# The low halves of FFN 1's first four weight blocks formed in PSUM, in a kernel with attention and two feed-forward nets

## The chip, the cores and the metric

The kernel runs on one core of a Trainium2 chip. The metric is the time of one execution in microseconds of device time, the median of the runs shown. The core has five engines with queues of their own: TensorE (PE in the profile, with its weight loads as PEld), VectorE (DVE), ScalarE (ACT), GpSimd (POOL) and SyncE (SP), which here only starts transfers. Each works through its own list in order, and waits at an instruction until what it needs is there.

## The reference

Attention over a sliding window, then two feed-forward nets, all in float32. What is computed, cut to what matters:

```python
# q, k, v: (4, 8, 576, 64); window 128, causal, with a slope per head
scores = scale * q @ k.T + slope[h] * -(abs(i - j))        # where 0 <= i - j < 128
attn = exp(scores - max) / (sum + 1e-9)
x = (attn @ v)            # laid out as 2304 tokens x 512
# FFN 1: w_in (512, 1024), w_out (1024, 512)
h = x @ w_in
solu = h * softmax(h)
ln = (solu - mean) / sqrt(var + 1e-6) * g_ln
y = ln @ w_out
# FFN 2: w_gate, w_val (512, 1536), w_out (1536, 512)
g = y @ w_gate
out = (g * sigmoid(g) * (y @ w_val)) @ w_out
```

## The kernel before

The weights of both nets arrive as float64 words and are decoded on the chip. For the big products every float32 operand is split into a high half (rounded to the type float32r, in which TensorE takes a 512-column product in one pass) and a low half (what the rounding left over). A product is then three passes: low by high, high by low, high by high (HALVES).

The tokens are worked in 18 chunks of 128 (numbered 0 to 17), and attention in each chunk in four pairs of heads. For a chunk and pair the steps are: `score` (line 518, TensorE), the row maxima with the bias (L571, VectorE), the exponentials (L597 for the chunks below SUMS, L606 for the others, ScalarE), for the chunks from SUMS on the division by the row sums (L576 and L577 on VectorE, L584 on GpSimd), the turning of the probabilities (L657, TensorE, for the chunks below TURN; through a DMA from TURN on), the copies out of PSUM (L667 on VectorE, L670 on ScalarE), and the products with the values (L705, TensorE). For the chunks below SUMS TensorE also spreads the inverse sums (L713), and ScalarE and VectorE multiply with them (L735, L738). Then the chunk's x is split (L318 on ScalarE, L324 on GpSimd or L322 on VectorE).

FFN 1 stands in `up` (L798, names shared, 24 matmuls of 512 columns for a chunk), its statistics (L821, L829 to L849, with the exponentials L832 and the squares L840 on ScalarE), `flip` (L903, eight transposes for a chunk, or through a DMA) and `down1` (L798, names wout and lnT). The weights of FFN 1 come in eight blocks each of w_in and w_out. `decode` makes one: ScalarE turns the two words of each number (L356, L360), VectorE shifts and joins them (L361, L362), GpSimd adds (L364), ScalarE or VectorE rounds to the high half (`high`, L318 or L319), and VectorE or GpSimd subtracts to get the low half (`low`, L322 or L324). A block is held in one of two buffers named db until its low half is made. For w_out there is a multiplication with g_ln between (L373). FFN 2 follows with L1169 (gate and value) and L1348 (output), from about 293 us to the end.

The order in which each engine's instructions stand is made by a planner in the kernel (the class Emitter) when the program is built: every step has a rank (the chunk's number plus an offset such as O_SPL or PW_IN), every way of doing it an engine and a planned cost, and the planner takes the step with the lowest rank among those that are ready in its own reckoning. B_DVE, B_ACT and the values ending in 0 shift steps between VectorE, ScalarE and GpSimd. The constants at the top of the file (lines 48 to 88) thus set the order of the whole program.

## Time and profile before

| | |
|---|---|
| time before, median of 3 runs | 717.71 us (716.42 to 717.73) |
| the profiled execution | 716.97 us, of which the span is 715.0 us |
| PE busy | 690.8 us, 97% of the span |
| PEld busy | 626.5 us, 88% |
| DVE, ACT, POOL busy | 559.4, 427.6 and 271.9 us |
| granted TensorE clock, mean | 0.995 |
| chain that ended last | PE 82%, DMA 8%, DVE 4% |

The span goes from the first instruction to the last. A busy PE need not be working at its full pace: the ends of matmuls are modelled in this view. In the rows further on, an arrow in an operation reads out of the right into the left (`pt<-bank`), `xN` is the number of records, and brackets hold the idle time before a row and what ended it.

### The profile page before, as it was taken

To read this page: it belongs to the slowest core of one execution; us is meant where nothing else is said; L and a number is where in the kernel's file an instruction comes from. 1 tells how busy PE (TensorE), PEld (TensorE's weight loads), DVE (VectorE), ACT (ScalarE), POOL (GpSimd) and SP (SyncE) were. 2 spreads that over 40 slices of the span, in tenths; PEclk is the share of its full clock that TensorE was granted. 3 is DMA by queue.
4 is the path that set the end of the run, shared out by engine and by line. 5 is a ranking of instruction groups with operands and counts; after the bars stand their busy time and mean duration, and the time that the engine had idled before them with its cause. 6 is when DMAs were issued, how large, how long until landed. Compare 5 with 4: busy or idle time off the path is not lost.

```text
span 715.0 us, 14190 instructions
## 1 busy us (share of the span) xinstructions
PE 690.8 (97%) x5060; PEld 626.5 (88%) x5060; DVE 559.4 (78%) x1458; ACT 427.6 (60%) x1019; POOL 271.9 (38%) x280
## 2 busy tenths in 40 slices
PE   3889999999999999999999999999999999999997
PEld 1666777788788888899999999999999999999997
DVE  6979995778877469968778677697794799886966
ACT  7899985755676357855565566465553663443432
POOL 2666899889987314700132132122210001200100
PEclk9999999999999999999999999999999999999999
DMA  9952158978878453437535445545441996886951
GB/s 315 352 159 65 46 147 214 249 207 197 190 188 181 86 147 97 125 92 139 185 130 172 145 155 162 171 161 185 155 148 54 370 378 220 262 287 204 311 166 67
DMA packets 113319, 130.24 MB, mean 182 GB/s; under 512 B 65632, under 2 KB 77920, under 8 KB 113248
## 3 DMA queue, kind: packets, MB, share of 16 engines
q1 hardware_dynamic: 112832, 128.87, 59.6%
q8 instruction: 40, 0.66, 0.4%
q10 hardware_dynamic: 416, 0.46, 0.2%
q14 instruction: 31, 0.25, 0.1%
HBM read 75.57 MB, written 39.06 MB: 160 GB/s over the span
## 4 chain that ended last, share of the span: by engine, by line
PE 82%; DMA 8%; DVE 4%; POOL 2%; ACT 2%; issue 1%; SPq 1%; ACTq 0%; POOLq 0%; DVEq 0%
PE bank L1169 32%; PE bank L798 26%; PE bank L1348 18%; PE bank L705 3%; PE bank L518 2%; DMA dw<-w 2%; DMA dw<-w_in 1%; DMA t<-yscr 1%; DMA dw<-w_out 1%; DMA keys<-qk 1%; PE bank L903 1%; DMA tables<-tables 1%; POOL shared L324 1%; POOL db L364 1%; PE bank L657 1%
## 5 line engine op out<-in xcount | busy, mean ns | idle before, releaser
L1169 PE MATMUL bank<-yt,w 128*128 128x384 f32 x1008 | 185.8, 337 | 0.4 <-ACT set L1191 0.4
L1169 PEld LDWEIGHTS bank<-yt,w 128*128 128x128 f32 x1008 | 176.2, 188 | 1.9 <-ACT set L1191 0.8
L364 POOL TENSOR_TENSOR db<-db,dw 128x512 int32<-128x512 int32 x52 | 73.7, 1419 | 204.4 <-DVE db L362 168.4
L1348 PE MATMUL bank<-w,wo 128*128 128x384 f32 x756 | 132.9, 337 | 1.2 <-POOL w L324 1.2
L1348 PEld LDWEIGHTS bank<-w,wo 128*128 128x128 f32 x756 | 132.3, 188 | 1.6 <-POOL w L324 1.6
L798 PE MATMUL bank<-wout,lnT 128*128 128x512 f32 x432 | 102.5, 391 | 0.0
L1169 PE MATMUL bank<-shared,w 128*128 128x384 f32 x504 | 97.2, 337 | 0.8 <-ACT set L1196 0.5
L798 PEld LDWEIGHTS bank<-wout,lnT 128*128 128x128 f32 x432 | 80.5, 188 | 16.8 <-issue 0.4
L1169 PEld LDWEIGHTS bank<-shared,w 128*128 128x128 f32 x504 | 88.4, 188 | 1.4 <-ACT set L1196 0.8
L798 PE MATMUL bank<-shared,shared 128*128 128x512 f32 x288 | 77.9, 406 | 0.9 <-POOL shared L324 0.6
L798 PEld LDWEIGHTS bank<-shared,shared 128*128 128x128 f32 x288 | 52.6, 191 | 14.4 <-issue 2.7
L606 ACT ACTIVATE e<-e,st 128x128 f32<-128x128 f32 x96 | 37.5, 400 | 22.9 <-DVE st L571 17.9
L318 ACT CAST w<-t 128x384 fp32r<-128x384 f32 (+2 forms) x35 | 26.3, 770 | 37.5 <-DVE t L1292 23.7
L356 ACT ACTIVATE dw<-dw 128x512 int32<-128x512 uint32 x52 | 34.8, 676 | 13.3 <-DMA dw<-w 11.0
L1203 ACT ACTIVATE set<-set 128x384 f32<-128x384 f32 x34 | 17.8, 525 | 40.3 <-DVE set L1201 40.3
L310 POOL COPY pl<-e 128x512 uint16<-128x512 uint16 (+1 forms) x50 | 39.9, 823 | 0.4
L322 DVE TENSOR_TENSOR w<-db,w 128x512 fp32r<-128x512 f32 (+1 forms) x48 | 30.7, 646 | 11.4 <-ACT w L318 11.0
L518 PE MATMUL bank<-keys,raw 64*32 64x160 f32 (+3 forms) x1152 | 30.0, 313 | 9.9 <-DMA raw<-qk 6.3
L361 DVE TENSOR_SCALAR db<-db 128x512 uint32<-128x512 uint32 x52 | 29.9, 576 | 11.7 <-ACT db L360 11.7
L798 PE MATMUL bank<-shared 128*128 128x512 f32 x144 | 38.7, 390 | 0.0
L362 DVE SCALAR_TENSOR_TENSOR db<-dw,db 128x512 uint32<-128x512 uint32 x52 | 36.9, 712 | 0.8
L318 ACT CAST w<-db 128x512 fp32r<-128x512 f32 (+1 forms) x45 | 25.4, 566 | 16.6 <-POOL db L364 7.3
(134 smaller groups left out, 1232.9 us busy)
## 6 DMA issues: line engine op xcount, KB each, us to landing
dw<-w SPq DMA_DIRECT2D x36, 512.0 KB, 4.6
t<-ascr SPq DMA_DIRECT2D x21, 768.0 KB, 6.0
ascr<-set SPq DMA_DIRECT2D x34, 384.0 KB, 2.9
later<-ascr SPq DMA_DIRECT2D x15, 768.0 KB, 6.0
wo<-wscr SPq DMA_DIRECT2D x6, 896.0 KB, 8.6
lscr<-pl SPq DMA_DIRECT2D x20, 256.0 KB, 2.9
v<-v SPq DMA_DIRECT2D x18, 256.0 KB, 3.6
yscr<-ys SPq DMA_DIRECT2D x18, 256.0 KB, 2.3
```

The lines of the kernel that those rows point to most:

```text
L310: (POOL, 100.0 + 1.72 * n, lambda: nc.gpsimd.tensor_copy(dst, words))]
L318: return [(ACT, t_act(n, sbuf), lambda: nc.scalar.copy(hi, src)), (DVEP if sbuf else DVE, t_dve(n, sbuf), lambda: nc.vector.tensor_copy(hi ...
L322: ways = [(DVEP if sbuf else DVE, t_dve(n), lambda: nc.vector.tensor_sub(lo, src, hi.bitcast(F32)))]
L356: r = yield (ACT, 48 + t_act(512), lambda: nc.scalar.activation(a, lw, AF.Copy, scale=2.0 ** -29), (), 0.0, O_DEC)
L361: x = yield (DVEP, t_dve(512, True), lambda: nc.vector.tensor_scalar(b, b, 3, None, ALU.logical_shift_left), [x], 0.0, O_DEC)
L362: x = yield (DVEP, t_dve(512), lambda: nc.vector.scalar_tensor_tensor(b, hw, 0x80000000, b, ALU.bitwise_and, ALU.bitwise_or), [x], 0.0, O_DEC)
L364: x = yield (POOL, 1290, lambda: nc.gpsimd.tensor_tensor(b.bitcast(I32), b.bitcast(I32), a, ALU.add), [x, r], 0.0, O_DEC)
L518: nc.tensor.matmul(banks[ks[r]][i:i + Q, j * 256 + o:j * 256 + o + w], raw[c][rows, 2 * qd + j, i:i + Q], kt[rows, 2 * qd + j, k0:k0 + w], ...
L606: ex.append((yield (ACT, 68 + 75 * j + t_act(P, True, True), lambda j=j: nc.scalar.activation(e[0:n, j], e[0:n, j], AF.Exp, bias=st[0:n, j ...
L798: nc.tensor.matmul(o, terms[m][0], terms[m][1], start=(m == 0), stop=(m == len(terms) - 1))
L1169: nc.tensor.matmul(o, l, r, start=first and m == 0, stop=m == 5, skip_group_check=True)
L1348: nc.tensor.matmul(o, w[:, b], ob[k, i][a][:, j], start=i == 0 and m == 0, stop=i == HB - 1 and m == 2)
```

## The change

Four of the eight blocks of w_in get their low half in another way. TensorE multiplies the decoded float32 block by the identity into a PSUM bank, and adds minus the identity times the high half; the bank then holds the low half, and ScalarE or VectorE copies it out. The planner leaves the choice between these two engines to its costs; it chose ScalarE for all four. One small tile `minus` is made once from the identity. The block's buffer is given back when TensorE has read it. All the constants that set the order are new.

```diff
-SUMS = 6
-TURN = 9
+SUMS = 5
+TURN = 10
-WHOLE = 10
+WHOLE = 9
-VB = 3
-PW_2 = -9.573
+VB = 4
+PW_2 = -11.369
...
+O_LO = -0.25
+BY_PE = 4
...
-    def decode(hi, lo, src, scale=None, even=False):
+    def decode(hi, lo, src, scale=None, even=False, by_pe=False):
...
         x = yield (high(hi, bf, 512), [x], 0.0, O_SPL)
+        if by_pe:
+            k = yield bank_s
+
+            def rest():
+                nc.tensor.matmul(banks[k], ident, bf, start=True, stop=False)
+                nc.tensor.matmul(banks[k], minus, hi, start=False, stop=True)
+
+            x = yield (PE, 1080, rest, [x] + minus_ok, 0.0, O_LO)
+            em.give(db_s, x)
+            x = yield ([(DVE, t_dve(512), lambda: nc.vector.tensor_copy(lo, banks[k])),
+                        (ACT, t_act(512, False), lambda: nc.scalar.copy(lo, banks[k]))], [x], 0.0, O_SPL)
+            em.give(bank_s, x, k)
+            yield x
+            return
         ways = low(lo, bf, hi, 512)
...
+    minus = at.tile([P, P], F32R, name="minus")
...
-                    yield from decode(win[0][:, r, cs], win[1][:, r, cs], w_in[r * P:(r + 1) * P, cs])
+                    yield from decode(win[0][:, r, cs], win[1][:, r, cs], w_in[r * P:(r + 1) * P, cs], by_pe=half * KM + r < BY_PE)
```

In the changed file the lines stand 2 lower from line 371 on and 20 lower behind the new code: L320 is the old L318, L358 and L362 the old L356 and L360, L538 the old L518, L617 the old L597, L677, L690, L725, L733 and L818 the old L657, L670, L705, L713 and L798. L382 and L383 are the two new matmuls, L388 is the new copy out of the bank, L465 makes `minus`.

SUMS moves chunk 5 to the other way of dividing by the sums, TURN moves the turning of chunk 9 from the DMA to TensorE. Over the whole program TensorE gets 8 more transposes (L657, 72 to 80), 8 fewer products with the sums (L713, 48 to 40) and the 8 new matmuls; VectorE makes 1 of w_in's low halves instead of 4 and GpSimd 3 instead of 4; VectorE also loses its 3 of the 16 bias tiles (L462), 5 of 6 copies L671 and 2 casts L319 of w_in, all to ScalarE. The two halves of a chunk's scores stand back to back 3 times instead of 11 times.

Here is TensorE's list behind the first scores (bank is PSUM, tables holds the identity, e the probabilities, db a decoded block, shared the halves of w_in and x, pt the turned probabilities). Before:

```order
32 L518 MATMUL bank_82<-keys,raw 32x128
33 L657 MATMUL bank_83<-tables,e 128x128 x2
34 L657 MATMUL bank_86<-tables,e 128x128 x2
35 L657 MATMUL bank_79<-tables,e 128x128 x2
36 L705 MATMUL bank_80<-pt,v 64x128 x4
37 L657 MATMUL bank_83<-tables,e 128x128 x2
38 L518 MATMUL bank_84<-keys,raw 32x160
```

And with the change:

```order
33 L382 MATMUL bank_80<-db,tables 128x512
34 L383 MATMUL bank_80<-shared_73,minus 128x512
35 L677 MATMUL bank_86<-tables,e 128x128 x2
36 L677 MATMUL bank_82<-tables,e 128x128 x2
37 L725 MATMUL bank_83<-pt,v 64x128 x4
38 L677 MATMUL bank_80<-tables,e 128x128 x2
39 L677 MATMUL bank_86<-tables,e 128x128 x2
```

The first low half stands ahead of the first turning; the other three stand between the scores of chunks 1 to 3, all ahead of the first `up`.

Next is ScalarE's list at its start (dw the words of a block, bias the bias tiles, rs the row sums). Before:

```order
6 L461 ACTIVATE bias<-tables 128x128 x13
7 L597 ACTIVATE e,rs<-e,st 128x128 x3
8 L356 ACTIVATE dw<-dw 128x512
9 L670 COPY pt<-bank_83 128x256
10 L360 ACTIVATE db<-dw 128x512
11 L597 ACTIVATE e,rs<-e,st 128x128 x3
12 L670 COPY pt<-bank_86 128x256
13 L597 ACTIVATE e,rs<-e,st 128x128 x2
14 L356 ACTIVATE dw<-dw 128x512
```

And with the change:

```order
6 L481 ACTIVATE bias<-tables 128x128 x2
7 L465 ACTIVATE minus<-tables 128x128
8 L481 ACTIVATE bias<-tables 128x128 x11
9 L320 CAST shared_73<-db 128x512
10 L481 ACTIVATE bias<-tables 128x128 x3
11 L358 ACTIVATE dw<-dw 128x512
12 L362 ACTIVATE db<-dw 128x512
13 L617 ACTIVATE e,rs<-e,st 128x128 x3
14 L388 CAST shared_74<-bank_80 128x512
15 L690 COPY pt<-bank_86 128x256
16 L617 ACTIVATE e,rs<-e,st 128x128 x2
```

All the bias tiles, the first high half and the first copy of a low half now stand in ScalarE's list among the first exponentials.

Last, TensorE's list up to the turning of chunk 6's fourth pair, the 28th pair to be turned (ident is the identity, e_948 a chunk of FFN 1). Before:

```order
325 L713 MATMUL bank_83<-tables,rs 64x128 x8
326 L657 MATMUL bank_84<-tables,e 128x128 x2
327 L657 MATMUL bank_79<-tables,e 128x128 x2
328 L657 MATMUL bank_86<-tables,e 128x128 x2
329 L798 MATMUL bank_81<-shared_73,shared_74 128x512 x2
330 L798 MATMUL bank_81<-shared_73 128x512 x4
331 L657 MATMUL bank_79<-tables,e 128x128 x2
332 L903 MATMUL bank_83<-ident,e_948 128x128 x4
```

And with the change:

```order
360 L725 MATMUL bank_85<-pt,v 64x128 x2
361 L725 MATMUL bank_85<-pt,vd 64x128 x2
362 L725 MATMUL bank_85<-pt,v 64x128 x2
363 L818 MATMUL bank_81<-shared_74,shared_73 128x512 x4
364 L818 MATMUL bank_81<-shared_73,shared_74 128x512 x2
365 L677 MATMUL bank_82<-tables,e 128x128 x2
366 L677 MATMUL bank_87<-tables,e 128x128 x2
367 L818 MATMUL bank_81<-shared_73,shared_74 128x512 x2
```

The same turning stands at row 331 before and at row 366 now: more of TensorE's work, 18 more matmuls of `up` among it, stands ahead of it.

## Rows read from the trace of the kernel before

**Rows 1.** Busy us per stretch: PE, PEld, DVE, ACT, POOL, then clock and DMA.
```profile
60.00:90.00 30.00, 29.33 (x369) 22.37 (x369) 28.76 (x117) 29.18 (x92) 22.70 (x25) 1.00 0.19 55
...
320.00:610.00 290.00, 287.53 (x1641) 285.39 (x1641) 226.78 (x405) 159.89 (x304) 51.91 (x41) 1.00 0.55 184
```

**Rows 2.** Timeline of all engines at the 28th turning (start us, length us).
```profile
83.84 0.40 ACT L606 ACTIVATE e<-e,st 128x128 f32<-128x128 f32 x1
...
84.33 0.16 DVE L576 TENSOR_SCALAR st<-bank 128x2 f32<-128x2 f32 x1
...
85.34 0.61 POOL L584 TENSOR_TENSOR e<-e,st 128x256 f32<-128x256 f32 x1
...
86.09 0.41 PE L657 MATMUL bank<-tables,e 128*128 128x128 f32 x2
```

**Rows 3.** Waits of ScalarE from 0 to 90 us (us in total, times, longest).
```profile
ACT dw L356 <- DMA dw<-w_in: 2.3, 1, 2.3
ACT e L597 <- DVE st L571: 2.3, 3, 1.3
ACT L356 <- issue: 1.7, 1, 1.7
ACT db L360 <- DVE shared L322: 1.0, 1, 1.0
ACT rec L735 <- PE bank L713: 1.0, 1, 1.0
ACT shared L318 <- POOL db L364: 0.9, 2, 0.8
...
ACT pt L670 <- DVE pt L667: 0.4, 2, 0.2
```

**Rows 4.** Chain that ended last, pieces on TensorE from 82 to 90 us (start, length).
```profile
83.10 0.87 PE bank L713 x16
...
86.50 0.87 PE bank L903 x8
87.37 0.70 PE bank L518 x32
88.07 1.02 PE bank L705 x16
```

**Rows 5.** The same from 200 to 260 us.
```profile
204.08 1.27 PE bank L518 x64
205.35 11.10 PE bank L798 x48
```

**Rows 6.** Timeline of ScalarE from 72 us on (start, length).
```profile
71.74 0.61 ACT L318 CAST wout<-db 128x512 fp32r<-128x512 f32 x1
72.25 0.67 ACT L360 ACTIVATE db<-dw 128x512 f32<-128x512 f32 x1
...
74.30 0.36 ACT L670 COPY pt<-bank 128x256 f32<-128x256 f32 x1
74.55 0.69 ACT L840 ACTIVATE bank<-e,mst 128x512 f32<-128x512 f32 x1
...
78.34 0.68 ACT L832 ACTIVATE e<-bank,mst 128x512 f32<-128x512 f32 x1
...
79.00 0.62 ACT L318 CAST wout<-db 128x512 fp32r<-128x512 f32 x1
```

**Rows 7.** Groups by line and shape (busy us, mean ns of one | idle before).
```profile
L318 ACT CAST shared<-bank 128x512 fp32r<-128x512 f32 x12 | 7.2, 598 | 10.7 <-PE bank L798 10.2 <-PE bank L705 0.3
L461 ACT ACTIVATE bias<-tables 128x128 f32<-128x128 f32 x13 | 2.7, 295 | 0.5 <-DMA tables<-tables 0.5
L322 DVE TENSOR_TENSOR shared<-db,shared 128x512 fp32r<-128x512 f32 x4 | 2.7, 685 | 0.0
```

**Rows 8.** Timeline of GpSimd and of TensorE at the first `down1`.
```profile
108.48 1.30 POOL L324 TENSOR_TENSOR wout<-db,wout 128x512 fp32r<-128x512 f32 x1
...
111.42 0.84 PE L798 MATMUL bank<-wout,lnT 128*128 128x512 f32 x3
```

More of the change, by code (lines that the diff above doesn't have):

```diff
@@ L49 @@
 PLB = 4
-SUMS = 6
-TURN = 9
+SUMS = 5
+TURN = 10
 PTB = 2
-WHOLE = 10
+WHOLE = 9
 VDB = 3
-VB = 3
-PW_2 = -9.573
-LEAD = 3.239
-R_FLIP = 1.841
-R_DOWN = 3.016
-PW_IN = [-1.723, -0.17, -0.332, -0.327, 0.64, 0.002, 0.561, -0.486]
-PW_OUT = 3.66
-B_DVE = 1919.181
-B_ACT = 1456.515
-B_DVE0 = 542.373
-B_ACT0 = 356.722
-EARLY = 30027.441
+VB = 4
+PW_2 = -11.369
+LEAD = 3.126
+R_FLIP = 1.491
+R_DOWN = 3.254
+PW_IN = [-2.019, -0.278, -0.411, -0.308, 0.634, -0.009, 0.561, -0.486]
+PW_OUT = 3.883
+B_DVE = 1917.394
+B_ACT = 1450.825
+B_DVE0 = 209.589
+B_ACT0 = -514.17
+EARLY = 26097.701
 HALVES = [(0, 1), (1, 0), (0, 0)]
 HB = NC2 // 2
-O_MAX = 1.15
-O_EXP = 0.594
-O_INV = -0.93
-O_TURN = -3.445
-O_PT = -2.255
-O_PL = -0.523
-O_VAL = -0.098
-O_X = -0.608
-O_SC = -1.263
-O_DEC = 0.971
-O_SPL = -0.547
-O_FLIP = -0.513
-O_LN = -2.53
-O_SET = -0.863
-O_FREE = -5.207
+O_MAX = 1.071
+O_EXP = 0.554
+O_INV = -0.894
+O_TURN = -3.268
+O_PT = -2.206
+O_PL = -0.828
+O_VAL = -0.054
+O_X = -0.522
+O_SC = -1.182
+O_DEC = 1.034
+O_SPL = -0.648
+O_LO = -0.25
+BY_PE = 4
+O_FLIP = 0.227
+O_LN = -2.504
+O_SET = -0.101
+O_FREE = -4.379
 TOGETHER = 76077.562
-PATIENCE = -715.862
-LEAST = 20
+PATIENCE = -1936.646
+LEAST = 22
 WARM, COOL = 3400.0, 1900.0
@@ L396, in attention_then_two_ffns @@
     base, ident = tables[:, 0:2 * P], tables[:, 2 * P:3 * P]
+    minus = at.tile([P, P], F32R, name="minus")
+    minus_ok = []
     tri = tables[:, 3 * P:5 * P].rearrange("p (j c) -> p j c", j=2)
@@ L446, in load @@
                 tri_ok.append((yield (DMA, 300.0, lambda: None, (), 400.0)))
+                minus_ok.append((yield ([(ACT, t_act(P), lambda: nc.scalar.activation(minus, ident, AF.Copy, scale=-1.0)),
+                                         (DVEP, t_dve(P), lambda: nc.vector.tensor_scalar_mul(minus, ident, -1.0))], [ident_ok[0]])))
                 late_ok.append((yield (POOL, 0.0, lambda: nc.gpsimd.tensor_copy(ident_late, ident), [tri_ok[0]])))
```

## The prediction

> **What bounds the kernel now.** The page says that TensorE is busy for 97% of the span and that the chain which ended last is 82% TensorE. I read the stretches first. From 320 to 610 us PE and PEld are both busy nearly all the time, 287.5 and 285.4 of 290 us [rows 1]. There TensorE is full, and a microsecond of work on it is a microsecond of the end. From 60 to 90 us it is otherwise: PE shows 29.33 of 30 us, but PEld only 22.37, while VectorE shows 28.76 and ScalarE 29.18 [rows 1]. So I looked at which wait ends last in that stretch. At the turning of chunk 6's fourth pair (the 28th) the reader sees a relay: the second exponential starts on ScalarE at 83.84 us, VectorE adds to the sum at 84.33, GpSimd multiplies from 85.34 to 85.95, and TensorE turns at 86.09 [rows 2]. TensorE comes on the heels of ScalarE's list. Behind that place TensorE's list runs on with hardly a gap, so the end is the time of the 28th turning plus what TensorE still has to do. That is the frame of the whole sum.
>
> The sum is made against the profiled execution: a span of 715.0 us, 716.97 us with what lies around it, 0.74 us under the median of 717.71. I add that difference back.
>
> **TensorE's work, part by part.** The four low halves add four float32 matmuls and four float32r matmuls of 512 columns. A float32r one takes 11.10 / 48 = 0.23 us [rows 5]. A plain float32 one of 512 columns is not in the trace. A transpose of 128 columns is one record of 0.87 / 8 = 0.109 us, and a plain float32 matmul is two records (eight in the list are sixteen in the trace: L713) [rows 4]. From below it is 4 x 0.109 = 0.44 us, as if one record did, from above twice the two-record price, 1.74 us, as if the clock stood at its lower level for all four. I take the two records, 0.87 us, since L713 has the same types. With the float32r one that is 1.10 a block and 4.4 us for four (2.7 to 7.9).
>
> Eight fewer products with the sums give back 0.87 us; eight more transposes cost 8 x 0.109 = 0.87 [rows 4]. Scores of both halves of a chunk in one go take 1.27 us [rows 5], apart twice 0.70 [rows 4]: eight partings of 0.13 are 1.0 us. The whole program thus has 4.4 - 0.9 + 0.9 + 1.0 = 5.4 us more on TensorE.
>
> Now the part ahead of the 28th turning. By the two lists there stand ahead of it: 18 more matmuls of `up` (4.2 us), the low halves (4.4), one more half of scores (0.7) and of values (1.0), eight more turnings of FFN 1 (0.9) and eight fewer products with the sums (-0.9), together 10.3 us [rows 4, 5]. So behind it 10.3 - 5.4 = 4.9 us less is left. The price of the low halves stands in both figures and falls out: as long as TensorE is the one that waits there, they cost nothing at the end, whichever bound is true.
>
> **ScalarE's work ahead of that turning.** By the lists the same 56 exponentials, and in addition nine casts or copies of 512 columns (four low halves, two high halves of w_in, two of FFN 1's turned values, one of x), four small tiles (three bias, one `minus`), five copies L670 and two exponentials L832. A cast is 72.25 - 71.74 = 0.51 us from start to start, a copy L670 0.25, an L832 with its sum 0.66 [rows 6], a small tile 2.7 / 13 = 0.21 [rows 7]. That is 4.6 + 0.8 + 1.3 + 1.3 = 8.0 us. The copy of a low half out of PSUM I price as the cast of x out of PSUM, whose mean of 598 ns [rows 7] is near the 0.61 of a cast from SBUF [rows 6]; by that row in full, not overlapped, nine of them are 5.4, so the 8.0 could be 8.8. From below the copies are free only if ScalarE idled in their place, which is the next term.
>
> **ScalarE's idle time.** With the same waits as before the turning would come 8.0 later and 4.9 less be left: an end 3.1 us later. But ScalarE waited 6.1 us behind its start: 2.3 for VectorE's maxima, 1.0 for a buffer held by VectorE's subtraction, 1.0 for L713, 0.9 for GpSimd's additions, 0.4 for VectorE's masks and small ones [rows 3]. The change takes the subtractions (0.685 us each [rows 7]), bias tiles, casts and copies from VectorE's early list, so its maxima stand further ahead of ScalarE's exponentials. I let go the buffer wait (1.0, the buffer is now given back by TensorE), the wait for L713 (1.0; by the lists more of ScalarE's work now stands ahead of L735), 1.4 of the 2.3 (the longest one, 1.3, hangs on chunk 1's scores, which wait for a transfer, and stays for 0.9), and 0.8 of the masks and small ones. The 0.9 for GpSimd stays. New: ScalarE's cast of chunk 0's x stands ahead of the fourth copy and waits for L738, which now stands behind a subtraction of v on VectorE, and the cast of the last of the four blocks waits for GpSimd; by the order of the lists I give these 0.7 together. Behind each such wait stand the exponentials of the next pairs, for which TensorE waits in turn. So 4.2 goes and 0.7 comes: 3.5 us less. The bounds are 0 (every wait that goes is replaced) and 5.3 (all but 0.8 goes).
>
> **The sum.** 8.0 - 4.9 - 3.5 = -0.4 us: a span of 714.6, and 717.3 us as a median. What goes on VectorE and GpSimd is covered: they are not on this path any more than now. SyncE's list keeps its first transfers (two chunks and all of w_in) in the same order, and the turning of chunk 9 leaves the DMA, two round trips fewer; neither is waited for at this place.
>
> One rule speaks to the reading. The Trainium skill (Trainium Kernel Development and Optimization, Performance Expectations) says that matmul busy time is a bad measure because matmuls are pipelined, and that the busy share of weight loads is a good one. By PE's row TensorE has 0.7 us free in 60 to 90 us, and an added 5.4 would come out as some 5 us at the end; by the rule's measure it has 7.6 us free and the addition hides in the stretches ahead. The relay at 86.09 us agrees with the rule. Against it, small weights load faster, so that share is low for scores and values even without waiting.
>
> **The rivals.**
> ScalarE hardly waits. With VectorE ahead, 5.3 of the 6.1 us go: 8.0 - 4.9 - 5.3 = -2.2, 715.5 us. For it speaks that three of the seven rows of waits, 3.7 us, name VectorE [rows 3]. Against it: GpSimd would become the next limit. The last low half of w_out ended at 109.78, and the first `down1` began at 111.42 [rows 8]. With the change GpSimd has 12.7 us more ahead of it by the lists (nine more divisions, five more copies, three more normalisations, less two low halves), so the low half comes at 122.5 if it idles as before, while `down1` has 18.4 us more of TensorE ahead, and would come at 111.4 + 18.4 - 5.4 = 124.4 with an unchanged end. So the gain stops at 1.9 us unless GpSimd idles less too.
>
> The other side: ScalarE waits as long as before, because its copies now hang on a TensorE that is itself waiting for ScalarE's exponentials. The place is the start: a copy of a low half waits for two matmuls that stand behind turnings. The price is the whole 3.1 us, 720.8 us. It decides as soon as ScalarE's idle time shrinks by less than 1.7 us. For it: the 1.0 us for L713 shows that ScalarE does wait for TensorE here. Against it: at each of the four copies other work stands between.
>
> That the change doesn't do what it says: the low halves leave VectorE, but most of the subtractions saved were not what ScalarE waited for. That is the middle of these two, within 0.2% of now.
>
> **How the numbers follow.** About 0.2%, 1.43 us, is what a measurement of this kernel can tell from no change. The forecast has 0.40, the rival with a gain 0.32, the one with a loss 0.28. The later waits of TensorE (2.5 of 290 us [rows 1]) may move by 1 us either way, so a part of each case falls over its bound: faster 0.34 (0.28 of the gain, 0.06 of the forecast), same 0.37, slower 0.29. For the forecast alone the range is 715.8 to 719.0; with both rivals and that microsecond it is 714.0 to 721.0.
>
> **What would show it.** Right: the 28th turning at about 86.1 + 8.0 - 3.5 = 90.6 us, on the heels of ScalarE; ScalarE's waits behind its start at 2.6 us; all new copies on ScalarE at about 0.6 us; the two matmuls of a block at 1.1 us. Wrong would be: a 28th turning later than 93, ScalarE's waits for TensorE above 2 us, a wait of TensorE for GpSimd's last low half of w_out, or a turning that TensorE reaches later than its inputs, which would make the 5.4 us count in full.

## The result, and the profile after

The changed kernel took 720.40, 720.53 and 722.02 us, and 1145.77 in a fourth, disturbed run that is left out of the comparison (with it the median is 721.27), against 717.07 before: a ratio of 1.0064, 95% interval 1.0044 to 1.0085. Run again it took 720.04 against 716.81, ratio 1.0047 (1.0030 to 1.0064). By the two ratios it is slower by 4.6 and 3.4 us; the forecast was no change. The profiled execution of the second measurement took 720.15 us, with a span of 718.3, that is 3.3 more than the 715.0 before. All rows of the changed kernel are from it.

Busy time by stretch, columns as in [rows 1]:

```profile
60.00:90.00 30.00, 29.76 (x321) 22.60 (x318) 29.11 (x119) 29.15 (x88) 24.57 (x27) 1.00 0.20 54
320.00:610.00 290.00, 288.00 (x1643) 285.76 (x1643) 225.97 (x405) 161.07 (x306) 53.29 (x42) 1.00 0.55 183
```

The picture of [rows 1] has not changed: TensorE is full from 320 us on, and from 60 to 90 us VectorE and ScalarE are as full as TensorE. Next the timeline at the 28th turning, which answers to [rows 2]:

```profile
89.36 0.40 ACT L626 ACTIVATE e<-e,st 128x128 f32<-128x128 f32 x1
...
90.14 1.05 POOL L312 COPY pl<-e 128x1024 uint16<-128x1024 uint16 x1
90.18 0.15 DVE L596 TENSOR_SCALAR st<-bank 128x2 f32<-128x2 f32 x1
...
91.14 0.62 POOL L604 TENSOR_TENSOR e<-e,st 128x256 f32<-128x256 f32 x1
...
91.70 0.60 PE L677 MATMUL bank<-tables,e 128*128 128x128 f32 x4
```

The last row holds the 27th and the 28th turning back to back; the 28th starts at 91.92, 0.16 us behind the end of GpSimd's division and 5.8 us later than before. The steps come in the order of [rows 2], but TensorE does not wait for them. Here are the weight loads of the turning, first before, then after:

```profile
86.06 0.20 PEld L657 LDWEIGHTS bank<-tables,e 128*128 128x128 f32 x2 [0.32 <-POOL e L584]
```

```profile
91.48 0.59 PEld L677 LDWEIGHTS bank<-tables,e 128*128 128x128 f32 x4
```

Before, the loads stood still for 0.32 us, but from the matmul ahead to the turning it was 0.31 us instead of the usual 0.23, so TensorE lost only 0.08. Now there is no gap at all. The last place ahead of the 28th turning at which TensorE's matmuls waited lies further back, first before, then after:

```profile
68.89 1.66 PE L798 MATMUL bank<-shared,shared 128*128 128x512 f32 x6 [0.35 <-ACT rec L735]
```

```profile
77.24 1.65 PE L818 MATMUL bank<-shared,shared 128*128 128x512 f32 x6 [0.18 <-DVE lnT L324]
```

From there TensorE works on to the 28th turning without another wait, for 17.2 us before and for 14.7 now. This last wait ends 8.35 us later than before, at another place of the list, and it is for VectorE instead of ScalarE; behind it 641.1 us are left instead of 646.1. On the chain that ended last, 26.8 of the 32.2 us from 45 us to this place are now VectorE's and 2.6 ScalarE's (before, 14.8 and 3.9 of the 23.9 us). The two stretches on either side of the 28th turning, first before, then after:

```profile
0.00:86.09 86.09, 68.94 (x879) 49.95 (x879) 74.61 (x295) 75.23 (x235) 50.63 (x49) 0.96 0.59 195
86.09:715.00 628.91, 621.88 (x4183) 576.59 (x4182) 484.81 (x1164) 352.41 (x785) 221.27 (x232) 1.00 0.60 180
```

```profile
0.00:91.92 91.92, 78.04 (x948) 53.86 (x949) 77.25 (x312) 83.14 (x259) 54.93 (x56) 1.00 0.57 185
91.92:718.30 626.38, 618.05 (x4118) 570.52 (x4116) 482.05 (x1140) 353.71 (x779) 209.78 (x220) 1.00 0.60 179
```

These four rows are the prediction's sum in measured form; as a split of the span it adds up at any place, and it does not show who waited for whom. ScalarE (fourth busy time) did 83.14 - 75.23 = 7.9 us more ahead of the turning and idled 8.8 us there instead of 10.9. Behind it TensorE had 621.88 - 618.05 = 3.8 us less to do, and idled 8.3 us instead of 7.0. ScalarE's waits behind its start, answering to [rows 3], and TensorE's waits from 90 to 200 us:

```profile
ACT pt L690 <- DVE pt L687: 1.1, 1, 1.1
ACT e L852 <- DVE mst L849: 1.0, 1, 1.0
ACT e L617 <- DVE st L591: 0.8, 1, 0.8
ACT db L375 <- POOL db L366: 0.5, 1, 0.5
ACT shared L320 <- DVE rec L758: 0.4, 1, 0.4
```

```profile
PE bank L725 <- POOL pt L661: 1.9, 1, 1.9
PE bank L725 <- DVE pt L659: 0.4, 1, 0.4
PE bank L725 <- DVE st L596: 0.3, 1, 0.3
```

ScalarE's waits add up to 3.8 us. VectorE's maxima (L591) went from 2.3 to 0.8, as forecast, but two other waits for VectorE came up: 1.1 (0.4 before) and 1.0 (none before). None is for a low half. TensorE's 1.9 us are new: before, its only waits there were 0.7 in all. They come from chunk 11, whose second turning through the DMA landed late:

```profile
177.22 1.27 POOL L661 TENSOR_TENSOR pt<-pt,tables 128x512 f32<-128x512 f32 x1 [2.58 <-DMA pt<-escr]
...
178.54 0.44 PE L725 MATMUL bank<-pt,vd 128*64 128x128 f32 x4 [1.88 <-POOL pt L661]
```

Last the new instructions: the fourth block, with TensorE at full pace, and the group of the copies (duration ns min/median/max):

```profile
30.99 1.02 PE L382 MATMUL bank<-db,tables 128*128 128x512 f32 x2
31.48 0.76 PE L383 MATMUL bank<-shared,minus 128*128 128x512 f32 x1
32.08 0.51 PE L677 MATMUL bank<-tables,e 128*128 128x128 f32 x2
```

```profile
L388 ACT CAST shared<-bank x4: 562/577/585, 13.1 to 32.8; 128x512 fp32r<-128x512 f32 x4
```

A plain float32 product of 512 columns is two records, and the fourth block takes 32.08 - 30.99 = 1.09 us (1.10 forecast); the third took 1.29, the second waited for a cast, and the first ran at TensorE's slower pace. A copy out of PSUM takes 0.58.

### The profile page after: what moved, and what is told of

It reads as the page before. It is cut to its first block, busy times and chain, and to the rows that moved or that the text cites. A ratio compares the mean times of both kernels' runs of the same rounds, so it can differ in the third digit from the quotient of the medians.

```text
span 1144.0 us, 14251 instructions
## 1 busy us (share of the span) xinstructions
PE 1129.8 (99%) x5064; PEld 771.1 (67%) x5064; DVE 562.9 (49%) x1451; ACT 445.5 (39%) x1037; POOL 259.4 (23%) x275
## 4 chain that ended last, share of the span: by engine, by line
PE 98%; DMA 2%; DVE 0%; POOL 0%; issue 0%
PE bank L1189 38%; PE bank L818 29%; PE bank L1368 19%; PE bank L725 5%; PE bank L538 3%; PE bank L677 1%; DMA dw<-w_in 1%; PE bank L923 1%; PE bank L733 1%; PE bank L382 0%; DMA keys<-qk 0%; POOL db L366 0%; PE bank L383 0%; DVE bank L584 0%; DVE set L1229 0%; DVE later L1383 0%
## 5 line engine op out<-in xcount | busy, mean ns | idle before, releaser
L1189 PE MATMUL bank<-yt,w 128*128 128x384 f32 x1008 | 301.4, 480 | 0.0
L1189 PEld LDWEIGHTS bank<-yt,w 128*128 128x128 f32 x1008 | 218.9, 217 | 72.6 <-issue 4.3
L1368 PE MATMUL bank<-w,wo 128*128 128x384 f32 x756 | 218.5, 479 | 0.6 <-DVE set L1229 0.6
L1368 PEld LDWEIGHTS bank<-w,wo 128*128 128x128 f32 x756 | 165.6, 219 | 53.2 <-DVE set L1229 1.2
L818 PE MATMUL bank<-wout,lnT 128*128 128x512 f32 x432 | 171.2, 577 | 0.0
L1189 PE MATMUL bank<-shared,w 128*128 128x384 f32 x504 | 156.2, 479 | 0.0
L818 PEld LDWEIGHTS bank<-wout,lnT 128*128 128x128 f32 x432 | 93.6, 218 | 69.1 <-issue 40.9
L818 PE MATMUL bank<-shared,shared 128*128 128x512 f32 x288 | 123.0, 582 | 0.0
L818 PEld LDWEIGHTS bank<-shared,shared 128*128 128x128 f32 x288 | 60.5, 217 | 42.8 <-issue 27.1
L818 PE MATMUL bank<-shared 128*128 128x512 f32 x144 | 61.7, 580 | 0.0
L320 ACT CAST w<-t 128x384 fp32r<-128x384 f32 (+2 forms) x35 | 26.0, 768 | 82.0 <-PE bank L1368 45.8
L1229 DVE TENSOR_TENSOR set<-set,bank 128x384 f32<-128x384 f32 x34 | 18.8, 554 | 66.2 <-PE bank L1189 66.2
L538 PE MATMUL bank<-keys,raw 64*32 64x160 f32 (+4 forms) x1152 | 40.4, 408 | 7.4 <-DMA raw<-qk 6.3
L818 PEld LDWEIGHTS bank<-shared 128*128 128x128 f32 x144 | 32.5, 225 | 22.3 <-issue 12.4
L1213 DVE TENSOR_TENSOR set<-set,bank 128x384 f32<-128x384 f32 x34 | 18.8, 554 | 57.1 <-PE bank L1189 40.3
L324 DVE TENSOR_TENSOR w<-db,w 128x512 fp32r<-128x512 f32 (+1 forms) x48 | 30.1, 633 | 29.7 <-ACT w L320 29.5
L324 DVE TENSOR_TENSOR w<-t,w 128x384 fp32r<-128x384 f32 (+2 forms) x34 | 29.1, 860 | 31.6 <-ACT w L320 31.6
```

The costliest lines, as they stand in the source:

```text
L320: return [(ACT, t_act(n, sbuf), lambda: nc.scalar.copy(hi, src)), (DVEP if sbuf else DVE, t_dve(n, sbuf), lambda: nc.vector.tensor_copy(hi ...
L324: ways = [(DVEP if sbuf else DVE, t_dve(n), lambda: nc.vector.tensor_sub(lo, src, hi.bitcast(F32)))]
L538: nc.tensor.matmul(banks[ks[r]][i:i + Q, j * 256 + o:j * 256 + o + w], raw[c][rows, 2 * qd + j, i:i + Q], kt[rows, 2 * qd + j, k0:k0 + w], ...
L818: nc.tensor.matmul(o, terms[m][0], terms[m][1], start=(m == 0), stop=(m == len(terms) - 1))
L1189: nc.tensor.matmul(o, l, r, start=first and m == 0, stop=m == 5, skip_group_check=True)
L1213: g1 = yield (DVE, t_dve(NH), lambda: nc.vector.tensor_add(t[:, 0], t[:, 0], sx), [x2, s1], 0.0, O_FREE)
```

## The experiments

Most kernels below keep the order of every instruction that they do not name: the planner still reckons with the old step, and only what is issued in its place differs. So they can be read against their parent step by step. "28th" is the start of the 28th turning in the profiled execution, "behind" what is left of the span after it. These two columns come from one execution each, and runs of one kernel lie 2 to 7 us apart; behind the 28th turning the seven kernels of the new order that do the same there (changed to after_no_lo) stand between 624.9 and 628.6. So a difference of a microsecond in these columns says nothing by itself.

| kernel | median us | ratio to before (95%) | 28th | behind |
|---|---|---|---|---|
| before | 716.4 to 717.1 | 1 | 86.09 | 628.9 |
| changed (after_clean) | 720.04 | 1.0047 (1.0030 to 1.0064) | 91.92 | 626.4 |
| lo_cheap | 722.03 | 1.0082 (1.0063 to 1.0100) | 92.69 | 627.2 |
| lo_double | 720.13 | 1.0056 (1.0037 to 1.0075) | 92.95 | 624.9 |
| evict_dve | 721.83 | 1.0086 (1.0058 to 1.0114) | 92.84 | 627.2 |
| sub_dve | 724.49 | 1.0119 (1.0083 to 1.0155) | 94.92 | 628.6 |
| sub_pool | 720.86 | 1.0065 (1.0045 to 1.0085) | 92.43 | 627.9 |
| after_no_lo | 722.96 | 1.0082 (1.0056 to 1.0107) | 92.42 | 628.2 |
| before_no_lo | 716.29 | 0.9996 (0.9975 to 1.0017) | 83.75 | 629.3 |
| kept_pe | 721.95 | 1.0078 (1.0054 to 1.0102) | 91.87 | 629.0 |
| kept_pe_dve | 720.43 | 1.0060 (1.0039 to 1.0081) | 90.31 | 629.1 |
| kept_pool | 717.99 | 1.0021 (1.0002 to 1.0040) | 87.38 | 630.9 |
| no_wait_11 | 721.35 | 1.0068 (1.0042 to 1.0093) | 92.23 | 628.0 |
| no_wait_all | 721.92 | 1.0069 (1.0046 to 1.0091) | 91.95 | 625.7 |
| loads_late | 722.28 | 1.0064 (1.0041 to 1.0087) | 92.46 | 627.8 |
| before_filled | 718.05 | 1.0018 (1.0004 to 1.0032) | 86.52 | 629.3 |
| before_filled_2 | 718.79 | 1.0031 (1.0015 to 1.0047) | 87.05 | 628.4 |

**The changed kernel again.** 

> The changed kernel once more, for a trace of it at full clock; about 721 us, ratio 1.006. By the theory that ScalarE waits as long as before (the rival with a loss), the 28th turning (L677) stands at about 94 us, on the heels of an exponential, and ScalarE's waits behind its start add up to about 6 us up to there. By the theory that TensorE comes to its turnings later than their inputs, so that its added 5.4 us count in full, the 28th turning starts right behind another TensorE instruction and ScalarE's waits there are well below 6 us. By the theory of GpSimd's last low half of w_out, TensorE waits 2 us or more at the first down1 for L326. By the theory of later waits, the three places agree with the forecast (28th turning near 90.6 us) and TensorE's waits behind 90 us grew by about 4 us.

None of these four fits whole. The turning is at 91.9, between the first theory's 94 and the forecast's 90.6. The second theory comes nearest: the turning starts right behind another TensorE instruction, and ScalarE's waits are 3.8 us; but the span grew by 3.3 and not by 5.4. One later wait of 1.9 us is there, half of what the last theory asks.

**What the low halves cost TensorE.** Two kernels change only the product of the identity with a block:

```diff
-                nc.tensor.matmul(banks[k], ident, bf, start=True, stop=False)
+                nc.tensor.matmul(banks[k], minus, hi, start=True, stop=False)    # lo_cheap
+                nc.tensor.matmul(banks[k], ident, bf, start=True, stop=True)     # lo_double: once more,
+                nc.tensor.matmul(banks[k], ident, bf, start=True, stop=False)    # overwritten
```

> The changed kernel, every instruction in its place, with the float32 product identity times block replaced by a second float32r product minus the identity times the high half (so the four low halves hold other numbers). By the rows of before TensorE's work falls by 4 x (0.87 - 0.23) = 2.6 us, ScalarE's and VectorE's stays. If TensorE's price falls out of the sum (ScalarE sets the 28th turning): as the changed kernel within 0.5 us, 721. If it counts in full: 718.7 us.

> The changed kernel, every instruction in its place; each product of the identity with a block is made twice in a row (the second overwrites the first), so TensorE has four float32 matmuls of 512 columns more, 3.5 us by two records each. If the price of the low halves on TensorE falls out: at most 0.5 us slower than the changed kernel, the 28th turning at 92 us. If it counts in full: 3.5 us slower, ratio 1.010. By what the cheaper form did (slower by 1 to 2 us, its first product waiting for the high half), the first product runs in the time of the cast to the high half; then the second, behind the cast's end, costs about 0.4 us a block at the most in the chain block, cast, products, copy.

Taking 2.6 us off TensorE made nothing faster, and adding 3.5 us (both by the prediction's prices) cost 1.0 us at the 28th turning and nothing that the times can tell. The price falls out, as the prediction had it. At the second block the reader sees why; first the changed kernel, then lo_double:

```profile
20.84 1.13 PE L382 MATMUL bank<-db,tables 128*128 128x512 f32 x2 [0.23 <-POOL db L366]
23.03 0.51 PE L383 MATMUL bank<-shared,minus 128*128 128x512 f32 x1 [1.06 <-ACT shared L320]
```

```profile
20.88 2.38 PE L382 MATMUL bank<-db,tables 128*128 128x512 f32 x4
23.07 0.50 PE L383 MATMUL bank<-shared,minus 128*128 128x512 f32 x1
```

The product with the block runs while ScalarE still casts the high half, and L383 needs that cast: it starts at 23.03 with the product once and at 23.07 with it twice. In lo_cheap both products need the high half, so nothing runs beside the cast: TensorE stands idle there for 2.43 us and is at its slower pace behind it, so lo_cheap takes off more than work. The prediction weighed a rule of the Trainium skill (Trainium Kernel Development and Optimization, Performance Expectations), by which the busy share of the weight loads and not that of the matmuls is the good measure of TensorE: as the prediction reads it, an added 5 us hides in the first 90 us. lo_double does not decide on it: its 3.5 us stand ahead of 33 us, where TensorE's matmuls themselves leave gaps. Where the prediction used the rule, between 60 and 90 us, the trace speaks against that reading. In the changed kernel's stretch from the last wait to the 28th turning (columns as in [rows 1]) the weight loads are busy for 75%, and still no room on TensorE is to be seen, since no matmul starts more than some 0.2 us behind its usual pace:

```profile
77.24:91.92 14.68, 14.68 (x146) 11.06 (x147) 14.47 (x61) 14.04 (x45) 12.43 (x15) 1.00 0.19 55
```

**The same low halves on another engine, or none.** In the new order: copied out by VectorE (evict_dve), subtracted on VectorE (sub_dve) or GpSimd (sub_pool) where TensorE formed them, left out (after_no_lo). In the old order: left out (before_no_lo), VectorE's four on GpSimd (kept_pool), formed in PSUM (kept_pe, kept_pe_dve).

```diff
-                        (ACT, t_act(512, False), lambda: nc.scalar.copy(lo, banks[k]))], ...
+                        (ACT, t_act(512, False), lambda: nc.vector.tensor_copy(lo, banks[k]))], ...    # evict_dve
...
-                nc.tensor.matmul(banks[k], ident, bf, start=True, stop=False)
-                nc.tensor.matmul(banks[k], minus, hi, start=False, stop=True)
+                nc.vector.tensor_sub(lo, bf, hi.bitcast(F32))    # sub_dve; nc.gpsimd in sub_pool; no copy
...
-            terms = [(xs[a][:, k], win[c][:, k, cs]) for a, c in HALVES for k in range(KM)]
+            terms = [(xs[a][:, k], win[c if cs.start else 0][:, k, cs]) for a, c in HALVES for k in range(KM)]    # no_lo
...
+                k = min(bank_s.free)[1]    # kept_pe, in place of the subtraction
+                nc.tensor.matmul(banks[k], ident, bf, start=True, stop=False)
+                nc.tensor.matmul(banks[k], minus, hi, start=False, stop=True)
+                nc.scalar.copy(lo, banks[k])
```

> The changed kernel with the same order; the four low halves are copied out of PSUM by VectorE at the same place in the program instead of by ScalarE. ScalarE's list loses 4 x 0.58 = 2.3 us ahead of the 28th turning, VectorE's gains about 4 x 0.6. If ScalarE's list sets the 28th turning: up to 2.3 us earlier, about 718 to 719. If ScalarE then waits for VectorE's maxima instead: no gain, 720 to 721, with ScalarE's waits for L591 longer. Slower (722 or more) if VectorE was as full as ScalarE.

> The changed kernel with the same order, but the four low halves are made by a subtraction on VectorE (four of 0.69 us) at the place where TensorE formed them; no matmuls, no copies out of PSUM. TensorE's work falls by 4.4 us, ScalarE's by 2.3, VectorE's list grows by 2.7. If the forming on TensorE is what costs: 4 us less than the changed kernel (716 to 717). If ScalarE's list sets the early part: 2 us less (718 to 719), at the price of VectorE's added work if its maxima come later. If the loss is made by the new order alone: within 0.5 us of the changed kernel.

> The changed kernel in its order, the four low halves made by GpSimd at the place where TensorE formed them (4 x 1.3 us on GpSimd; no matmuls, no copies out of PSUM, so ScalarE loses 2.3 us and TensorE 4.4, VectorE nothing). If ScalarE's list sets the 28th turning: up to 2 us faster than the changed kernel, 718 to 719. If GpSimd's list does as VectorE's did (4 us slower): 722 to 725. If the loss is made by the new order alone and these four hardly matter: 720 to 721.

> The changed kernel in its order without the low halves of the first four blocks: no matmuls, no copies out of PSUM for them, and the products of the first half of FFN 1 take the high halves in their place (other numbers, the same products in size and count). TensorE has 4.4 us less, ScalarE 2.3, nothing is added anywhere. The difference to the changed kernel is the whole price of forming them there. If ScalarE's list sets the start: 718, 2.3 us less. If TensorE's work counts: 716. If every microsecond taken from ScalarE comes back as a wait, as in the kernels that moved the work to VectorE or GpSimd: 719.5 to 720.5. What is then left over the next kernel is the price of the new order.

> The kernel before in its order without the low halves of the same four blocks (three subtractions on VectorE, one on GpSimd; the products take the high halves). The difference to the kernel before is the whole price that the change could have saved. If VectorE's subtractions were what the start waited for: 714.5 to 715.5. If they were covered: 716.5 to 717. Together with the kernel just described: if the new order makes the loss, that one stays 3 us or more above this one; if the forming makes it, they are within 1 us.

> The kernel before in its own order, VectorE's four low halves of w_in made on GpSimd at the same place (about 1.3 us each instead of 0.69): nothing on TensorE or ScalarE changes. If VectorE's list holds the start back: faster, 714 to 716. If ScalarE's list does: the same, 716 to 717.5. If GpSimd is as full as they are (it divides, and adds in decode): slower, 718 to 721.

> The kernel before in its own order; the low halves of the first four blocks of w_in are formed on TensorE at the place where VectorE (three) and GpSimd (one) subtracted, and copied out by ScalarE at the same place; one small tile minus. VectorE's list loses 2.1 us, ScalarE's gains 2.5, TensorE's 4.4. If the new order makes the loss of the change and the forming as such is a gain (by 4 us in the changed kernel against a subtraction on VectorE): 714 to 717. If the forming costs what it takes on ScalarE: 718 to 720. If it counts in full on TensorE: 721.

> The same with the four blocks whose low halves VectorE made (VectorE loses 2.7 us, ScalarE gains 2.5, TensorE 4.4). If VectorE's list is what the start hangs on: faster than the kernel before, 714 to 716. If ScalarE's is: slower, 718 to 720. If both are equally full: 716 to 718.

In the new order none of the four is faster than the changed kernel, not even the one that leaves the work out. So there the 2.3 us of copies and the 4.4 us on TensorE do not show in the time. Leaving the low halves out in the old order saves nothing that the runs can tell either (its runs spread from 714.4 to 719.3; the profiled one, of 715.2, had the turning 2.3 us earlier). With no low halves at all for the four blocks, the new order still is 722.96 / 716.29 = 1.009 of the old one. **The loss is there without the forming: it comes with the new order.** The expectation that ScalarE's list alone sets the 28th turning fell: four kernels took 2.3 us off it, and in none did the turning come earlier (it came 0.5 to 3.0 us later). The traces show why: in every kernel of the table in the new order TensorE's last wait ahead of the 28th turning is the one for VectorE's L324, at 77.2 to 80.2 us, and the turning follows 14.7 us later without a gap; in every one in the old order it is the one for ScalarE's copy of the spread sums (L735), 17.2 us ahead of the turning. What moves the turning happens ahead of that wait. kept_pool, which relieves VectorE in the old order, was slower by 1.3 us at the turning; ScalarE waited 2.2 us there for a buffer held by GpSimd's subtractions. ScalarE at one such place, first in the changed kernel, then in after_no_lo:

```profile
24.85 0.58 ACT L388 CAST shared<-bank 128x512 fp32r<-128x512 f32 x1
25.45 0.37 ACT L690 COPY pt<-bank 128x256 f32<-128x256 f32 x1
...
27.18 0.59 ACT L755 COPY rec<-bank 128x512 f32<-128x512 f32 x1
```

```profile
25.80 0.37 ACT L690 COPY pt<-bank 128x256 f32<-128x256 f32 x1 [0.74 <-DVE pt L687]
...
28.11 0.59 ACT L755 COPY rec<-bank 128x512 f32<-128x512 f32 x1 [0.47 <-PE bank L733]
```

The copy stood in a gap in which ScalarE would have waited for VectorE.

In the old order forming costs 3.9 to 7.3 us in kept_pe and 2.8 to 5.8 in kept_pe_dve (their intervals), all of it ahead of the 28th turning, and for the most part by the mechanism of the prediction's rival with a loss. ScalarE's waits from 9 to 92 us in kept_pe:

```profile
ACT shared L382 <- PE bank L381: 4.5, 4, 1.9
ACT rec L744 <- PE bank L722: 1.4, 2, 1.2
```

There ScalarE waits 4.5 us for the low halves (L382 is the copy). Another part can be the place of the small tile `minus`, which in both kernels stands at the head of ScalarE's list and waits for the tables:

```profile
7.05 0.31 ACT L454 ACTIVATE minus<-tables 128x128 fp32r<-128x128 f32 x1 [4.04 <-DMA tables<-tables]
```

So the first exponential starts at 10.96 instead of 9.61 us, and up to 1.35 us of the loss belong to that place and not to the copies. In the changed kernel the wait for the low halves is zero: the new order made room for the copies, and lost about as much elsewhere.

**The planner's own answers.** Only the constants were exchanged, and the planner ordered anew.

```diff
-BY_PE = 4
+BY_PE = 0    # after_no_pe: the new constants, no forming
...
-SUMS = 5
-TURN = 10
+SUMS = 6
+TURN = 9    # before_with_pe: these and all the other old constants, BY_PE = 4, O_LO = -0.25
```

> The changed kernel with all its new constants, but all low halves made on VectorE or GpSimd again (BY_PE 4 to 0). TensorE has 4.4 us less work and ScalarE five copies and small tiles less (about 2.6 us). If TensorE's added work counts in full: 721.3 - 4.4 = 717 us. If ScalarE's list sets the early part and TensorE's price falls out: ScalarE's 2.6 us go, less what VectorE's subtractions bring back as waits, 718.5 to 721. If the loss is made by the new constants (order, chunk 5's division, chunk 9's turning), it stays at 721.

It took 729.71 (1.0174, 1.0154 to 1.0195), above every number expected.

> The kernel before with its own constants, and the four low halves formed on TensorE (BY_PE 4, O_LO -0.25, nothing else new). TensorE gets 4.4 us more. If that counts in full: 722 us. If the start is set by ScalarE and TensorE's price falls out: 717.7 plus ScalarE's added copies (up to 4 x 0.6 us), less the subtractions that VectorE no longer makes, 716 to 720. If the loss of the change is made by the other constants: 717 to 718.

With the old constants and BY_PE = 4 it took 723.34 (1.0093, 1.0078 to 1.0108). Both are slower than either kernel: each half of the change alone costs more than both together. By what is not shown: everything moved, so they tell no part apart.

**The new wait at 178 us.** The first two let products read the first half's turned probabilities, in chunk 11 or in all chunks from 10 on; the third moves two loads on SyncE.

```diff
-    both[c, r // 2][:, late, ...]
+    both[c, 0 if c == 11 else r // 2][:, late, ...]    # no_wait_11; c >= TURN in no_wait_all
...
-        return (DMA, nbytes / 345.0, lambda: by.dma_start(dst, src), deps, 220.0)
+        return (DMA, nbytes / 345.0, lambda: put.append((dst, src)) if put_off else by.dma_start(dst, src), deps, 220.0)    # loads_late
```

> The changed kernel, every instruction in its place; only the products with the values of chunk 11's second half read the first half's turned probabilities (so 64 columns' worth of chunk 11 hold other numbers), and TensorE no longer waits there for the second turning through the DMA (the wait of 1.88 us at 178.54 us for L661). If the loss behind the 28th turning is that wait: 1.5 to 1.9 us less than the changed kernel, ratio to before about 1.003. If TensorE waits for something else instead a few us later, or if the whole loss lies ahead of the 28th turning: no gain, 1.005 to 1.006.

> The changed kernel, every instruction in its place; the products with the values of all chunks from 10 on read for their second half the first half's turned probabilities (other numbers), so that no product waits for a second DMA turning. If the late turnings cost what TensorE waits for them between 150 and 200 us: 1.5 to 2.6 us less than the changed kernel, 717.5 to 718.5. If TensorE then waits there for something else: 720 to 721.

In loads_late put_off is set for chunk 16, and what was put off is issued right behind the second DMA turning of chunk 11.

> The changed kernel; on SyncE two transfers, the queries and keys of chunk 16, stand behind the second DMA turning of chunk 11 instead of ahead of it, all else in place. That turning is issued about 1.2 us earlier and has 512 KB less beside it. If the wait of 1.88 us at 178.5 us is that transfer's and costs what it says: 718 to 719, 1 to 2 us less than the changed kernel. If a wait of the same size comes up at the next chunk (as at 190 us when the wait was taken away): 720 to 721.

The wait for L661 went in all three, and none is faster. TensorE's waits from 92 to 200 us in no_wait_11 and in no_wait_all:

```profile
PE bank L725 <- DVE ys L956: 2.0, 1, 2.0
PE bank L677 <- POOL e L604: 0.6, 1, 0.6
PE bank L725 <- DVE pt L659: 0.4, 1, 0.4
```

```profile
PE bank L725 <- DVE ys L956: 1.4, 1, 1.4
PE bank L725 <- DVE st L596: 0.4, 1, 0.4
PE bank L538 <- DVE ys L956: 0.3, 1, 0.3
```

Some 10 us later the next products wait 1.4 to 2.5 us for VectorE's copy of y (L956). TensorE has run ahead there of what feeds it, and when one wait is taken away it stands a little later for another.

**TensorE's pace.** In after_no_lo TensorE's records run at half the pace up to 29 us. I took that for the reason why leaving work out did not help, and put idle products into the old kernel's gaps.

```diff
             def flip_p():
+                for _ in range((0, 4, 5).count(u)): nc.tensor.matmul(banks[k], ident, tables[:, 0:512], start=True, stop=True)
...
         def scores():
+            for _ in range(2 if c == 1 and qd == 0 else 0): nc.tensor.matmul(banks[ks[0]], ident, tables[:, 0:512], start=True, stop=True)
```

> The kernel before with its low halves on VectorE and GpSimd; five float32 products of the identity with a table (512 columns each, overwritten by what follows) are put into TensorE's early gaps: one ahead of the turnings of pairs 0, 4 and 5, two ahead of the scores of chunk 1. No other engine gets anything. Theory: what the four low halves do for TensorE in the changed kernel is that its records run at full pace from 21 us on (16 records of the spread sums in 1.04 us against 1.92 without them), and any work in the gaps does that. Then the first L713 of this kernel falls to about 1.04 us for 16, scores of 32 records at about 26 us from 1.32 to 0.78, the 28th turning comes 1 to 2 us earlier, and the time is 714.5 to 716. If ScalarE and VectorE alone set the start: 716.5 to 717. If the added products delay the turnings: 718 or more.

> The same with nine of them: one ahead of the turnings of pairs 0, 1, 2 and 4, two ahead of pair 5, three ahead of the scores of chunk 1. If full pace is all that matters: as with five or up to 0.5 us faster. If the turnings of pairs 1, 2 and 5 do not wait as long as the products take (0.9 us each at full pace, some 2 us at half pace): 1 to 2 us slower than with five.

TensorE in before_filled (its line numbers stand 1 or 2 higher than before's: L715 is L713, L659 is L657):

```profile
21.06 1.04 PE L715 MATMUL bank<-tables,rs 128*64 128x128 f32 x16
...
23.65 0.33 PE L659 MATMUL bank<-tables,e 128*128 128x128 f32 x1 [0.49 <-ACT e L598]
25.04 0.33 PE L659 MATMUL bank<-tables,e 128*128 128x128 f32 x1 [1.06 <-ACT e L598]
```

The pace came as expected, the time did not: the turnings wait for the exponentials as before, and the kernel is 0.2% slower. This theory fell in the old order. In the new order it is not tested: lo_cheap, sub_dve and sub_pool ran at the slower pace like after_no_lo (16 records of L733 in 1.84 to 1.92 us), lo_double and evict_dve at full pace like the changed kernel (1.04), and no kernel leaves the work out and keeps the pace. So part of what leaving out might have saved can have gone to the pace; how much is not shown. No kernel here beats the one before.

## Why the prediction was wrong

| step | predicted | measured |
|---|---|---|
| ScalarE's work ahead of the 28th turning | +8.0 | +7.9 |
| ScalarE's idle time there | -3.5 | -2.1 |
| start of the 28th turning | 90.6 | 91.92 |
| TensorE's work left behind it | -4.9 | -3.8 |
| TensorE's idle time behind it | 0, +-1 | +1.3 |
| span | -0.4 | +3.3 |

**The path.** The step that failed is the reading that TensorE waits at the 28th turning and "comes on the heels of ScalarE's list", so that ScalarE's work and idle time set the turning and VectorE stays off the path. The gap of the weight loads there was 0.32 us, of which TensorE lost 0.08; its last wait was 17.2 us further back, at 68.89 us. In the changed kernel the last wait ends at 77.24 us, 8.35 us later, and it is for VectorE. From there TensorE's own work leads to the turning at 91.9 us without a gap, which is close to the prediction's last sign of being wrong: TensorE reaches the turning no sooner than its inputs are there. The 5.4 us did not count in full even so, since the low halves stand ahead of the last wait. Behind the last wait the span has 5.05 us less, and 8.35 - 5.05 = 3.3 is the loss. That ScalarE's work came out at 7.9 is a right count of its list, and no proof that the list sets the turning.

In the terms of the sum three were off, each by 1.1 to 1.4 us and all to one side; the two behind the turning are known to about a microsecond (TensorE's work there is 617.9 to 619.1 us in the seven kernels of the new order that do the same there).

**ScalarE's idle time.** The step said that "4.2 goes and 0.7 comes". The maxima, the buffer and L713 went as it said; but 1.7 us of waits for VectorE came up elsewhere (L687 and L849), where it had allowed 0.7 for two other places. The prediction took VectorE off the path because subtractions left it; the last wait at 77.24 us is for VectorE, and in sub_dve, with four subtractions of 0.69 us back on it, that wait ends 3.0 us later.

**The work left.** The step priced a parting of the scores at 0.13 us. It left out that whatever is parted also cuts the long runs of FFN 1's products: behind the turning these stand in 35 runs instead of 27. Within a run it is 0.227 us from start to start in both kernels; the first and the last product of a run take 0.15 us more together. So 18 products fewer save 178.7 - 176.4 = 2.3 us instead of the 4.2 reckoned. Scores and values save 1.8, and transposes cancel.

**The later waits.** The range gave them a microsecond either way; they took 1.3, most of it in one place that the prediction didn't name, and three kernels showed no gain from taking that wait away.

Right were the prices (1.09 and 0.58 us against 1.10 and 0.6), that the price of the low halves on TensorE falls out (in the changed kernel, as they stand ahead of the last wait), and ScalarE's +8.0. GpSimd's last w_out low half held nothing up: TensorE shows no wait for it. The rival with a loss gave 720.8, nearly the time measured, but that is luck: its mechanism did not happen in the changed kernel; it did in kept_pe.

What stays open: which of the new constants makes the last wait 8.35 us later. Each moves the whole list, and a kernel with one of them undone would be a third order, not a part of this one.

## What to carry to other kernels

Before a sum is built on the place where an engine waits, look whether that engine's own work loses time there, and go back to the last place where it does. Where three engines are equally full in a stretch, a microsecond taken off one is no gain until the wait that comes up in its place is named; leave the work out altogether, in either order, and see what is left over, before pricing a better way of doing it. A change that brings its own order is two changes: keep the order and exchange only the instruction to tell them apart. And more, shorter runs cost TensorE time, here 0.15 us a run; count the runs.

## What the runs showed of the hardware

TensorE's records ran at half the pace where the profile's granted clock says 1.00. From 24 to 28 us the column reads 1.00 in the changed kernel and in after_no_lo, yet the same two groups took, in this order:

```profile
24.88 0.66 PE L725 MATMUL bank<-pt,v 128*64 128x128 f32 x8
25.37 1.04 PE L733 MATMUL bank<-tables,rs 128*64 128x128 f32 x16
```

```profile
25.23 1.12 PE L725 MATMUL bank<-pt,v 128*64 128x128 f32 x8
26.14 1.92 PE L733 MATMUL bank<-tables,rs 128*64 128x128 f32 x16
```

From start to start of the two groups it is 0.49 against 0.91 us, a ratio of 1.86, near that of the two levels, 2.4 and 1.2 GHz. At 16 us both kernels were still at the slower pace, first the changed kernel, then after_no_lo:

```profile
16.25 1.12 PE L677 MATMUL bank<-tables,e 128*128 128x128 f32 x4
```

```profile
16.36 1.12 PE L677 MATMUL bank<-tables,e 128*128 128x128 f32 x4
```

The changed kernel's records come at full pace from 20.84 us on, those of after_no_lo from 29.24 on. Ahead of that the products of the first low half stood from 9.28 us on in the changed kernel, where TensorE in after_no_lo was idle for 3.53 us. The column does fall elsewhere: in the kernel before it reads 0.50 from 26 to 28 us, and 32 records of scores take 1.32 us there, as they do in after_no_lo at 27.99 us under 1.00.

The Trainium skill (TensorE: Matmul & The Clock Gate, Part 1) says that the array is throttled by default and that activity releases it; the durations agree, the granted clock in these rows does not show it. So a matmul's own row is the safer witness of the pace.
